# Scores laid out bank by bank with 12 matmuls per group, first queries in two loads, and VectorE exponentials in every sixth chunk

## The chip, the cores and the metric

One core of a Trainium2 chip runs the whole kernel. The metric is the device time of one execution in microseconds (us). Ratios compare versions on the same chip and in the same rounds. Spans in the profile are some 1.7 us shorter than the times.

## The reference

```python
B, Hq, Hkv, Sq, Sk, D = 16, 32, 8, 288, 512, 128      # bf16 q, k, v
k = jnp.repeat(k, rep, axis=1); v = jnp.repeat(v, rep, axis=1)   # rep = 4
scores = jnp.einsum("bhqd,bhkd->bhqk", q, k) * D ** -0.5
p = softmax(scores, axis=-1)
return jnp.einsum("bhqk,bhkd->bhqd", p, v)
```

The four query heads of one key head make a group: 128 groups of 4 x 288 = 1152 query rows, which are NT = 9 tiles of 128, against NJ = 4 key tiles of 128. A group has 36 blocks of 128 x 128 scores, or 4608 score columns, and is worked on in NC = 3 chunks of CH = 1536 columns, which are three banks each of PSUM, the memory that matmuls write to. There are NS = 384 chunks.

## The kernel before

Each step n of TensorE makes the scores of chunk n and the value matmuls of chunk n - 3. ScalarE takes the exponentials of a chunk in one instruction. In every ninth chunk VectorE takes the last 120 columns instead, by a polynomial in eight small operations. Row sums come from a column of ones beside the values, and VectorE divides as it evicts, that is, as it moves the results out of PSUM. Condensed, with comments added and lines left out:

```python
TPC = 3; BANK = 512; CH = TPC * BANK; LAG = 3; W = 120; EVERY = 9; FIRST_SHARED = 4
NPT = 6                                   # probability buffers; score buffers: 2
TW = TPC * P                              # 384: a chunk is [key tile j][3 query tiles]
cuts = sorted(set(range(0, CH + 1, BANK)) | set(range(0, CH + 1, TW)))
pieces = [(c, c // TW, c % TW, e - c) for c, e in zip(cuts[:-1], cuts[1:])]   # 384 128 256 256 128 384

def op_s(n):                              # scores of chunk n
    waits = [have("k", g), have_q(g, i)]
    if n >= 2: waits.append(("s_e", n - 1))            # exponential n-2 done: buffer free
    for x, (c, j, r0, w) in enumerate(pieces):
        if shared(n) and c + w == CH: w -= W           # the last W go elsewhere, by op_sy
        ins = matmul(ps_s[:, n % 2, c:c + w], kt_sb[..., j, gi, :], qg[:, r0:r0 + w])

def op_pv(r):                             # values of chunk r: 4 key tiles x 3 query tiles
    waits = [("s_vc", g + 1), ("s_e", r + 1), ("s_ev", r - 1)]
    ...
def op_q0(i):                             # first queries: three loads of three tiles
    c0, c1 = i * TPC, (i + 1) * TPC
    nc.sync.dma_start_transpose(qt_sb[:, 0, c0:c1], q_v[0:P, c0 * D:c1 * D])
# SP: q0(0) q0(1) q0(2) q(1) k(0, groups 2..3) q(2) v(groups 2..3) q(3) ...
# ACT queue: keys of group 0, then of group 1, then values of groups 0 and 1
for n in range(NS):                       # TensorE
    op_s(n)
    if shared(n): op_sy(n)
    if n == 2: op_kt(1, range(NJ), 1)     # transposes of group 1's keys
    if n >= LAG: op_pv(n - LAG)
```

## Time and profile before

| | before |
|---|---|
| time | 525.38 us (525.32 to 526.12, 3 runs) |
| step of TensorE | 1335 ns: scores 655, values 680 |
| ScalarE, one whole chunk, end to end | 1343.5 ns; with VectorE's help 1243 |
| scores of chunk 3 start | 9.07 us |
| from there to the end of the last scores ("steady part") | 508.22 us |

The lines that carry the reading are in the prediction below. Two more groups are useful (line, engine, operation, tiles and shapes, count, then busy us and mean ns of one, then idle time of the engine before them and what ended it): the value matmuls, which the change leaves alone, and VectorE's evictions, which share their engine with the polynomial.

```profile
L418 PE MATMUL ps_o<-v_sb,pt_sb 128*128 128x129 bf16 x4596 | 322.8, 220 | 0.2 <-DVE o_sb L522 0.2
L522 DVE TENSOR_TENSOR o_sb<-ps_o,rl_sb 128x384 bf16<-128x384 f32 x383 | 212.9, 556 | 10.3
```

The 0.2 us is the whole of what value matmuls waited for evictions, and it belongs to the tail.

### The profile page before, as it was taken

The page shows a single profiled execution, that of the slowest core. Times are in us where ns is not written, and L with a number is a line of the kernel's source. Part 1 is how long each engine was busy: PE and PEld are TensorE (multiplying, and loading weights), DVE is VectorE, ACT ScalarE, POOL GpSimd, SP SyncE. Part 2 cuts the span into 40 slices and gives each one's busy share as a digit, 9 for nine tenths or more (in the row PEclk, how much of TensorE's full clock was granted, in tenths as well). Part 3 has the DMA queues.
Part 4 walks back from the last instruction along what each step waited for, and adds up shares of the span by engine and source line. Part 5 has one row for each costly group of instructions (what it writes and reads, how often), then busy time and mean ns, then how long its engine had stood idle before and what let it go on. Part 6 is the DMA issues. An engine that isn't in the chain of part 4 may idle for free.

```text
span 523.5 us, 16876 instructions
## 1 busy us (share of the span) xinstructions
PE 517.6 (99%) x6981; PEld 459.0 (88%) x6981; DVE 339.9 (65%) x1148; ACT 515.1 (98%) x389; POOL 79.6 (15%) x135
## 2 busy tenths in 40 slices
PE   7999999999999999999999999999999999999997
PEld 5888888888888888888888888888888888888886
DVE  2766666666666666666666666666666666666665
ACT  6999999999999999999999999999999999999996
POOL 1111111111111111111111111111111111111110
PEclk9999999999999999999999999999999999999999
DMA  8999999999999999999999999999988999896212
GB/s 167 223 255 246 205 223 252 194 205 245 252 196 275 208 211 248 215 225 219 216 228 221 222 203 252 230 184 246 225 218 211 233 211 201 219 212 178 79 69 92
DMA packets 253147, 110.15 MB, mean 210 GB/s; under 512 B 219792, under 2 KB 236816, under 8 KB 253072
## 3 DMA queue, kind: packets, MB, share of 16 engines
q1 hardware_dynamic: 252512, 108.56, 97.7%
q8 instruction: 55, 0.90, 0.7%
q10 hardware_dynamic: 560, 0.52, 0.4%
q14 instruction: 20, 0.16, 0.1%
HBM read 17.04 MB, written 37.75 MB: 105 GB/s over the span
## 4 chain that ended last, share of the span: by engine, by line
PE 97%; DMA 1%; SPq 1%; DVE 0%; issue 0%
PE ps_o L418 50%; PE ps_s L384 47%; DMA qt_sb<-in_q_dram 1%; SPq L315 1%; PE ps_o L394 0%; DVE o_sb L522 0%; DVE rl_sb L512 0%; DVE o_sb L532 0%; PE ps_o L607 0%; DVE bad_sb L558 0%; DVE flag_i L675 0%; DVE bad_sb L555 0%
## 5 line engine op out<-in xcount | busy, mean ns | idle before, releaser
L453 ACT ACTIVATE pt_sb<-ps_s 128x1536 bf16<-128x1536 f32 (+2 forms) x385 | 512.8, 1455 | 0.6 <-PE ps_s L384 0.5
L418 PE MATMUL ps_o<-v_sb,pt_sb 128*128 128x129 bf16 x4596 | 322.8, 220 | 0.2 <-DVE o_sb L522 0.2
L384 PE MATMUL ps_s<-qt_sb,kt_sb 128*128 128x128 bf16 (+3 forms) x2304 | 312.2, 272 | 1.5 <-DMA qt_sb<-in_q_dram 1.4
L418 PEld LDWEIGHTS ps_o<-v_sb,pt_sb 128*128 128x128 bf16 x4596 | 289.9, 98 | 22.9 <-DVE o_sb L522 0.4
L384 PEld LDWEIGHTS ps_s<-qt_sb,kt_sb 128*128 128x128 bf16 x2304 | 193.4, 98 | 35.6 <-issue 1.0
L522 DVE TENSOR_TENSOR o_sb<-ps_o,rl_sb 128x384 bf16<-128x384 f32 x383 | 212.9, 556 | 10.3
L512 DVE RECIPROCAL rl_sb<-ps_o 128x3 f32<-128x3 f32 x383 | 68.7, 179 | 160.8 <-PE ps_o L418 160.8
L505 POOL COPY v_sb<-vd_sb 128x512 bf16<-128x512 bf16 x128 | 78.7, 615 | 431.6 <-PE ps_o L418 412.2
L486 DVE SCALAR_TENSOR_TENSOR u_sb<-u_sb,m_sb 128x120 f32<-128x120 f32 x84 | 23.4, 278 | 0.0
L493 DVE SCALAR_TENSOR_TENSOR pt_sb<-u_sb,e_sb 128x120 bf16<-128x120 f32 x42 | 12.2, 290 | 1.4
L486 DVE SCALAR_TENSOR_TENSOR u_sb<-m_sb 128x120 f32<-128x120 f32 x42 | 11.6, 277 | 0.0
L464 DVE TENSOR_SCALAR y_sb<-ps_o 128x120 f32<-128x120 f32 x42 | 10.6, 253 | 0.0
L477 DVE TENSOR_SCALAR m_sb<-t_sb 128x120 int32<-128x120 int32 x42 | 9.4, 223 | 1.4
L477 DVE TENSOR_SCALAR e_sb<-t_sb 128x120 int32<-128x120 int32 x42 | 9.5, 226 | 0.0
L394 PE MATMUL ps_o<-qt_sb,kt_sb 128*128 128x120 bf16 x42 | 9.1, 216 | 0.0
L470 DVE TENSOR_SCALAR t_sb<-y_sb 128x120 int32<-128x120 f32 x42 | 9.0, 213 | 0.0
L364 DVE COPY kt_sb<-ps_o 128x512 bf16<-128x512 bf16 x2 | 0.8, 424 | 6.6 <-PE ps_o L357 6.6
L394 PEld LDWEIGHTS ps_o<-qt_sb,kt_sb 128*128 128x128 bf16 x42 | 4.1, 98 | 0.0
L370 PE MATMUL ps_o<-z_sb 128*128 128x512 bf16 (+1 forms) x9 | 2.7, 447 | 1.3 <-DVE z_sb L638 1.3
L548 DVE TENSOR_REDUCE st_sb<-rl_sb 128x1 f32<-128x72 f32 (+1 forms) x16 | 3.5, 217 | 0.0
L550 DVE TENSOR_REDUCE st_sb<-rl_sb 128x1 f32<-128x72 f32 (+1 forms) x16 | 3.5, 216 | 0.0
L447 ACT ACTIVATE pt_sb<-ps_s 128x512 bf16<-128x512 f32 x1 | 0.6, 597 | 2.3 <-PE ps_s L384 2.3
(31 smaller groups left out, 11.6 us busy)
## 6 DMA issues: line engine op xcount, KB each, us to landing
out_dram<-o_sb SPq DMA_DIRECT2D x127, 288.0 KB, 4.0
vd_sb<-in_v_dram SPq DMA_DIRECT2D x31, 512.0 KB, 5.3
qt_sb<-in_q_dram SPq DMA_TRANSPOSE x130, 4.8
kt_sb<-in_k_dram SPq DMA_TRANSPOSE x32, 5.2
out_dram<-o_sb SPq DMA_DIRECT2D x3, 96.0 KB, 1.8
kd_sb<-in_k_dram ACTq DMA_DIRECT2D x2, 128.0 KB, 2.2
vd_sb<-in_v_dram ACTq DMA_DIRECT2D x1, 256.0 KB, 3.0
vd_sb<-in_v_dram SPq DMA_DIRECT2D x1, 256.0 KB, 3.4
```

Source lines behind the costliest of these rows:

```text
L384: ins = emit(eng, waits if x == 0 else [], lambda: eng.matmul(ps_s[:, n % 2, c:c + w], kt_sb[:, sl, j, gi, :], qg[:, r0:r0 + w], start=Tru ...
L394: emit(eng, [("s_ev", n - LAG - 1)], lambda: eng.matmul(ps_o[:, (n - LAG) % 2, BANK - W:BANK], kt_sb[:, (g // UG) % NSLOT, NJ - 1, g % UG, :],
L418: ins = emit(eng, w_x, lambda: eng.matmul(outs(r)[:, a, :], pt_sb[:, r % NPT, j, a * P:(a + 1) * P], v_sb[:, sl, gi * NJ + j, 0:DV], start ...
L453: emit(eng, waits, lambda: eng.activation(d, s, ACTF.Exp, scale=scale)).then_inc(sem["s_e"], 1)
L464: emit(eng, [("s_yb", nth(n) - NB), ("s_pv", n - LAG + 1)], lambda: eng.tensor_scalar(out=y_sb[:, b], in0=ps_o[:, (n - LAG) % 2, BANK - W: ...
L470: emit(eng, [("s_ym", 2 * (nth(n) - NB)), ("s_y", nth(n))], lambda: eng.tensor_scalar(out=t_sb[:, b], in0=y_sb[:, b], scalar1=Y_MUL, scala ...
L477: emit(eng, [("s_yp", nth(n) - NB), ("s_yb", nth(n))], lambda: eng.tensor_scalar(out=dst[:, b], in0=t_sb[:, b], scalar1=mask, scalar2=bits ...
L486: lambda: eng.scalar_tensor_tensor(out=u_sb[:, b, x], in0=src, scalar=QUARTIC[x], in1=m, op0=ALU.add, op1=ALU.mult)
L493: lambda: eng.scalar_tensor_tensor(out=pt_sb[:, n % NPT, NJ - 1, TW - W:TW], in0=u_sb[:, b, 2], scalar=QUARTIC[3], in1=e_sb[:, b].bitcast( ...
L505: emit(eng, waits, lambda: eng.tensor_copy(v_sb[:, sl, gi * NJ:(gi + 1) * NJ, 0:D], vd_sb[:, sl, gi].rearrange("p (j d) -> p j d", d=D))). ...
L512: emit(eng, [("s_pv", r + 1)], lambda: eng.reciprocal(rl_sb[:, TPC * r:TPC * (r + 1)].unsqueeze(2), outs(r)[:, :, D:DV])).then_inc(sem["s_ ...
L522: emit(eng, waits, lambda: eng.tensor_tensor(out=o_sb[:, g % NO, t0:t0 + TPC, :], in0=outs(r)[:, :, 0:D], in1=rl_sb[:, TPC * r:TPC * (r + ...
```

## The change

The diff is shortened ("..."), and its comments are added. The intent is to make the same scores with fewer matmuls, to let ScalarE keep up by giving VectorE more chunks to help in, and to get through the start with one transfer less. Scores of four query tiles against one key tile now fill a bank exactly: eight banks of 512 columns per group, and one bank with the ninth query tile against the four key tiles. A chunk is three consecutive banks. Therefore a value matmul may need exponentials of its own chunk and of the next.

```diff
-    EVERY = 9
+    EVERY = 6
-    FIRST_SHARED = 4
+    FIRST_SHARED = 6
-    TW = TPC * P
+    TB = BANK // P
+    NF = NT // TB * TB
...
-            c0, c1 = i * TPC, (i + 1) * TPC
+            c0, c1 = ((0, TB), (TB, NT))[i]            # first queries: 4 and 5 tiles
...
-        cuts = sorted(set(range(0, CH + 1, BANK)) | set(range(0, CH + 1, TW)))
-        pieces = [(c, c // TW, c % TW, e - c) for c, e in zip(cuts[:-1], cuts[1:])]
+        def place(t, j):
+            b, c = (t // TB * NJ + j, t % TB * P) if t < NF else (NF // TB * NJ + t - NF, j * P)
+            return b // TPC, b % TPC * BANK + c
+        def pieces(i):
+            left = [(place(t, j)[1], j, t, TB * P) for t in range(0, NF, TB) for j in range(NJ) if place(t, j)[0] == i]
+            return left + [(place(t, j)[1], j, t, P) for t in range(NF, NT) for j in range(NJ) if place(t, j)[0] == i]
...
-            waits = [("s_vc", g + 1), ("s_e", r + 1)]
+            waits = [("s_vc", g + 1), ("s_e", g * NC + uses(r % NC) + 1)]
...
-            op_kt(0, range(NJ), 0)
-            op_warm(8, P, ps_s[:, 1])
+            op_kt(0, range(1), 0)                      # first key tile alone, then the other three
+            op_kt(0, range(1, NJ), 1)
+            op_warm(5, P, ps_s[:, 1])
```

Cut: the same change of indices in the reading of the probabilities and in the polynomial's destination, the waits that free a probability buffer, and the copies that go with the split key transposes.

More of the change, by code (lines that the diff above doesn't have):

```diff
@@ L209, in bass_standalone__gqa_softmax__near_ridge_kernel @@
             S("s_o%d" % i)
-        for i in range(NC):
+        for i in range(2):
             S("s_qp%d" % i)
@@ L240, in bass_standalone__gqa_softmax__near_ridge_kernel @@
         kt_sb = main.enter_context(nc.sbuf_tensor("kt_sb", [P, NSLOT, NJ, UG, P], BF16))
-        pt_sb = main.enter_context(nc.sbuf_tensor("pt_sb", [P, NPT, NJ, TW], BF16))
+        pt_sb = main.enter_context(nc.sbuf_tensor("pt_sb", [P, NPT, CH], BF16))
         o_sb = main.enter_context(nc.sbuf_tensor("o_sb", [P, NO, NT, D], BF16))
@@ L318, in have_q @@
             if g == 0:
-                return ("s_qp%d" % i, 16)
+                return ("s_qp%d" % min(i, 1), 16)
             return ("s_q%d" % (g % NQ), 16 * (g // NQ + (0 if g % NQ == 0 else 1)))
@@ L325, in have @@
             if u == 0 and kind == "k":
-                return ("s_k%d" % min(g, 2), (1, 1, 16)[min(g, 2)])
+                return ("s_k%d" % min(g, 2), (2, 1, 16)[min(g, 2)])
             if u == 0:
@@ L345, in stored, with uses, used, pt @@
             return [("s_o%d" % (g % NO), 16 * (g // NO + 1)) for g in range(NG - NO, LASTG)] + [("s_ol", 16 * NC)]
-        cuts = sorted(set(range(0, CH + 1, BANK)) | set(range(0, CH + 1, TW)))
-        pieces = [(c, c // TW, c % TW, e - c) for c, e in zip(cuts[:-1], cuts[1:])]
+        def place(t, j):
[4 more added lines that the diff above has]
+            return left + [(place(t, j)[1], j, t, P) for t in range(NF, NT) for j in range(NJ) if place(t, j)[0] == i]
+        def uses(b):
+            return max(place(t, j)[0] for t in range(b * TPC, (b + 1) * TPC) for j in range(NJ))
+        def used(i):
+            return max(b for b in range(NC) for t in range(b * TPC, (b + 1) * TPC) for j in range(NJ) if place(t, j)[0] == i)
+        def pt(g, t, j):
+            i, c = place(t, j)
+            return pt_sb[:, (g * NC + i) % NPT, c:c + P]
         def op_kt(g, tiles, bank):
@@ L379, in op_s @@
                 waits.append(("s_e", n - 1))
-            qg = qt_sb[:, g % NQ, i * TPC:(i + 1) * TPC].rearrange("d t p -> d (t p)")
-            for x, (c, j, r0, w) in enumerate(pieces):
+            qg = qt_sb[:, g % NQ].rearrange("d t p -> d (t p)")
+            todo = pieces(i)
+            for x, (c, j, t, w) in enumerate(todo):
                 if shared(n) and c + w == CH:
                     w -= W
-                ins = emit(eng, waits if x == 0 else [], lambda: eng.matmul(
-                    ps_s[:, n % 2, c:c + w], kt_sb[:, sl, j, gi, :], qg[:, r0:r0 + w], start=True, stop=True))
+                w_x = waits if x == 0 else []
+                if n == 0 and x < 2:
+                    w_x = [("s_k0", 1), waits[1]] if x == 0 else waits[:1]
+                ins = emit(eng, w_x, lambda: eng.matmul(
+                    ps_s[:, n % 2, c:c + w], kt_sb[:, sl, j, gi, :], qg[:, t * P:t * P + w], start=True, stop=True))
                 if n == 0 and c + w == BANK:
@@ L392, in op_sy @@
             eng = nc.tensor
-            g, t = n // NC, n % NC * TPC + TPC - 1
+            g = n // NC
+            (t, j), = [(t, j) for t in range(NT) for j in range(NJ) if place(t, j) == (n % NC, CH - P)]
             emit(eng, [("s_ev", n - LAG - 1)], lambda: eng.matmul(
-                ps_o[:, (n - LAG) % 2, BANK - W:BANK], kt_sb[:, (g // UG) % NSLOT, NJ - 1, g % UG, :],
+                ps_o[:, (n - LAG) % 2, BANK - W:BANK], kt_sb[:, (g // UG) % NSLOT, j, g % UG, :],
                 qt_sb[:, g % NQ, t, P - W:P], start=True, stop=True))
@@ L415, in op_pv @@
                     w_x = waits if a == 0 and j == 0 else []
-                    if a == TPC - 1 and j == NJ - 1 and shared(r):
-                        w_x = w_x + [("s_yp", nth(r))]
+                    t = r % NC * TPC + a
+                    i, c = place(t, j)
+                    if c == CH - P and shared(g * NC + i):
+                        w_x = w_x + [("s_yp", nth(g * NC + i))]
                     ins = emit(eng, w_x, lambda: eng.matmul(
-                        outs(r)[:, a, :], pt_sb[:, r % NPT, j, a * P:(a + 1) * P],
+                        outs(r)[:, a, :], pt(g, t, j),
                         v_sb[:, sl, gi * NJ + j, 0:DV], start=(j == 0 and a == 0), stop=(j == NJ - 1),
@@ L429, in op_pv_last @@
                 ins = emit(eng, [("s_e", NS + (0 if a < TPC - 1 else 1))], lambda: eng.matmul(
-                    outs(NS - 1)[:, a, :], pt_sb[:, (NS - 1) % NPT, j, a * P:(a + 1) * P],
+                    outs(NS - 1)[:, a, :], pt(LASTG, NT - TPC + a, j),
                     v_sb[:, sl, gi * NJ + j, 0:DV], start=(j == 0), stop=(j == NJ - 1)))
@@ L439, in op_exp @@
             if n >= NPT:
-                waits.insert(0, ("s_pv", n - NPT + 1))
-            dst, src = pt_sb[:, n % NPT], ps_s[:, n % 2].rearrange("p (j r) -> p j r", r=TW)
-            parts = [(dst.rearrange("p j r -> p (j r)"), ps_s[:, n % 2])]
+                m = n - NPT
+                waits.insert(0, ("s_pv", m // NC * NC + used(m % NC) + 1))
+            d, s = pt_sb[:, n % NPT], ps_s[:, n % 2]
+            parts = [(0, CH)]
             if shared(n):
-                parts = [(d[:, 0:CH - W], s[:, 0:CH - W]) for (d, s) in parts]
+                parts = [(0, CH - W)]
             if n == 0:
-                d, s = parts[0]
                 emit(eng, [("s_s0", 1)], lambda: eng.activation(d[:, 0:BANK], s[:, 0:BANK], ACTF.Exp, scale=scale))
-                parts = [(d[:, BANK:CH], s[:, BANK:CH])]
+                parts = [(BANK, CH)]
             if n == NS - 1:
-                w = TW - P
-                parts = [(dst[:, :, 0:w], src[:, :, 0:w]), (dst[:, :, w:TW], src[:, :, w:TW])]
+                parts = [(0, CH - BANK), (CH - BANK, CH)]
+            parts = [(d[:, a:e], s[:, a:e]) for (a, e) in parts]
             for (d, s) in parts:
@@ L491, in op_yp @@
             eng, b = nc.vector, nth(n) % NB
-            emit(eng, [("s_pv", n - NPT + 1), ("s_ym", 2 * nth(n)), ("s_yu", 3 * nth(n))],
+            emit(eng, [("s_pv", (n - NPT) // NC * NC + used((n - NPT) % NC) + 1), ("s_ym", 2 * nth(n)), ("s_yu", 3 * nth(n))],
                  lambda: eng.scalar_tensor_tensor(
-                     out=pt_sb[:, n % NPT, NJ - 1, TW - W:TW], in0=u_sb[:, b, 2], scalar=QUARTIC[3],
+                     out=pt_sb[:, n % NPT, CH - W:CH], in0=u_sb[:, b, 2], scalar=QUARTIC[3],
                      in1=e_sb[:, b].bitcast(FP32), op0=ALU.add, op1=ALU.mult)).then_inc(sem["s_yp"], 1)
@@ L560, in op_over @@
                 op0=ALU.is_lt, op1=ALU.add)).then_inc(sem["s_bad"], 1)
-        first = [lambda i=i: op_q0(i) for i in range(NC)]
+        first = [lambda i=i: op_q0(i) for i in range(2)]
         first += [lambda: op_q(1), lambda: op_k(0, 2), lambda: op_q(2), lambda: op_v(0, None, 2, UG), lambda: op_q(3)]
@@ L640, in _ @@
             eng.memset(one_f[:], 1.0)
-            op_kc(0, range(NJ), 0, 1)
-            op_kc(1, range(NJ), 1, 2)
+            op_kc(0, range(1), 0, 1)
+            op_kc(0, range(1, NJ), 1, 2)
+            op_kc(1, range(NJ), 1, 3)
             per_b = G * NC
```

## The prediction

> **What bounds the kernel now.** I read the page's rows of busy time and its chain first, then the groups by shape, then the chain piece by piece in the steady part, and the start and the end last. Two engines look full:
>
> ```profile
> PE 517.6 (99%) x6981; PEld 459.0 (88%) x6981; DVE 339.9 (65%) x1148; ACT 515.1 (98%) x389; POOL 79.6 (15%) x135
> ...
> PE 97%; DMA 1%; SPq 1%; DVE 0%; issue 0%
> ```
>
> So the bound is TensorE or ScalarE, within a per cent, and the chain says TensorE. The work is 384 chunks of 1536 score columns: 3 per group, 128 groups. In each step TensorE makes the scores of chunk n (6 matmuls) and then the 12 probability-by-value matmuls of chunk n-3, while ScalarE takes the exponentials of a chunk. The rows by shape:
>
> ```profile
> L453 ACT ACTIVATE pt_sb<-ps_s 128x1536 bf16<-128x1536 f32 x340 | 461.5, 1467 | 0.6 <-PE ps_s L384 0.5
> L384 PE MATMUL ps_s<-qt_sb,kt_sb 128*128 128x384 bf16 x726 | 236.7, 326 | 1.5 <-DMA qt_sb<-in_q_dram 1.4
> L384 PE MATMUL ps_s<-qt_sb,kt_sb 128*128 128x128 bf16 x768 | 168.2, 219 | 0.0
> L384 PE MATMUL ps_s<-qt_sb,kt_sb 128*128 128x256 bf16 x768 | 146.6, 273 | 0.0
> L394 PE MATMUL ps_o<-qt_sb,kt_sb 128*128 128x120 bf16 x42 | 9.1, 216 | 0.0
> ```
>
> Durations of pipelined matmuls overlap, so the chain's pieces are the better measure of a step (start, length, what):
>
> ```profile
> 33.27 0.66 PE ps_s L384 x6
> 33.92 0.68 PE ps_o L418 x12
> 34.60 0.60 PE ps_s L384 x6
> 35.20 0.05 PE ps_o L394
> 35.26 0.68 PE ps_o L418 x12
> ```
>
> From the starts of single matmuls in the trace, one to the next: 162.5 ns after a 384-column one, 109.1 after 256, 55.9 after 128, 56.7 after 129 columns. The six scores take 2 x 162.5 + 2 x 109.1 + 2 x 55.9 = 655 ns and the twelve others 680; steps start 1335 ns apart, always, and the engine's idle time in the steady part is 0. Which engine leads is seen on ScalarE: each exponential begins a constant 49 ns after the modelled end of the last score matmul, and starts too are 1335 ns apart. But its single durations climb over eight chunks from 1444 to 1494 ns, and drop to 1402 when VectorE takes 120 columns (every ninth chunk). ScalarE's ends are thus 1343.5 ns apart: alone it is slower than TensorE. After the shared chunk it has caught up. Over nine chunks ScalarE needs 8 x 1343.5 + 1243 = 11,991 ns and TensorE 12,018, so TensorE leads by 27 ns in 12,018. The score buffers are double, so the next but one chunk still finds its buffer free about 300 ns early. A faster TensorE alone could gain only those 27 ns per nine chunks before ScalarE leads, 1.2 us in all; beyond that the two must go down together.
>
> The start is the second place. TensorE idles until the queries of group 1 have landed:
>
> ```profile
> 0.82 3.90 SPq L315 DMA_TRANSPOSE qt_sb<-in_q_dram  x3
> 4.77 1.43 SPq L310 DMA_TRANSPOSE qt_sb<-in_q_dram  x1
> ...
> 7.16 0.81 PE L384 MATMUL ps_s<-qt_sb,kt_sb 128*128 128x384 bf16 x6 [0.58 <-DMA qt_sb<-in_q_dram]
> 7.81 0.39 PE L357 MATMUL ps_o<-ident,kd_sb 128*128 128x128 bf16 x4
> 9.07 0.81 PE L384 MATMUL ps_s<-qt_sb,kt_sb 128*128 128x384 bf16 x6 [0.87 <-DMA qt_sb<-in_q_dram]
> ```
>
> From 9.07 us on, the scores of chunk 3, TensorE never stops until the tail at 518.5.
>
> **What the Trainium skill says.** "TensorE: Matmul & The Clock Gate", section "Wait — 56ns, not 53.3ns?": a warm matmul of N columns is followed by the next after N / 2.4 GHz plus about 2.5 ns, whatever N is (55.6 ns at 128 columns, 215.7 at 512). The trace agrees: 55.9, 109.1 and 162.5 are 53.3, 106.7 and 160 plus 2.4 to 2.6. "PSUM — Partial Sum Buffer", "The four PSUM rules": one matmul's output stays within one bank of 512 fp32 columns. That is why the old layout, 384 columns per key tile, had to be cut six times over three banks. "ScalarE: Activation LUTs", "What ACT_TABLE_LOAD costs": 0.833 ns per column, with successive ACTIVATEs overlapping. The trace has (1343.5 - 1243) / 120 = 0.84. "DMA: Bandwidth & Descriptors", "Issuing engines are not separate DMA queues": a second issuer saves only issue time, and all transfers share the 16 DMA engines; in the trace the first piece of the queries landed 1.2 us after its issue ended and the second, with keys and values under way, 2.1.
>
> **The change part by part.**
> Score matmuls. A group's 36 blocks of 128 columns are laid out anew: eight banks of one key tile by four query tiles (512 columns) and one bank with the ninth query tile (4 x 128). Per group that is 8 + 4 = 12 matmuls against 18, with the same 4608 columns. With 215.8 ns for 512 (213.3 + 2.5; the trace of before has no warm one), chunks 0 and 1 of a group cost 647.5 ns, chunk 2 costs 431.6 + 223.6 = 655. The mean is 650, a saving of 5 ns a step: 6 matmuls x 128 groups x 2.5 ns = 1.92 us. Everything lies on TensorE's path. From chunk 3 to chunk 383 it is 380 steps: 1.9 us.
>
> Sharing. 62 chunks instead of 42 (chunks 6, 12, ... 372). On TensorE a shared chunk has one more matmul, 20 x 2.5 ns = +0.05 us. On ScalarE each saves 100.5 ns, 2.0 us in all, which does not come off the end, but lets ScalarE follow: per six chunks 5 x 1343.5 + 1243 = 7960 ns, against TensorE's 6 x 1330 + 2.5 = 7983. TensorE still leads by 23 ns. With the old sharing ScalarE's 11,991 per nine chunks would have stood against TensorE's 11,973, so the new matmuls would have been held up by about 2 ns a step (0.8 us in all). VectorE pays eight small operations a chunk, 2.04 us by the sum of their rows, 20 x 2.04 = 41 us more on an engine busy for 340 of 523. Beside the matmuls, it has room: in a shared step its evictions end at least 0.8 us before TensorE wants the accumulator again, and 1.0 us elsewhere.
>
> New dependences. Values of query tiles now need exponentials of the next chunk (tile 0's last key tile is in chunk 1). The value matmuls of chunk n-3 come right after the scores of chunk n, which themselves waited for exponential n-2, so nothing waits longer. The probability buffers are freed one step later than before; with six of them the exponential wants one two steps after that.
>
> Start. Three query loads become two (4 and 5 tiles). Each of the three took 1.23 to 1.31 us to issue, and the whole of group 1 with nine tiles 1.43, so the issue hardly depends on size, and group 1 is issued 1.25 us earlier. The bytes stay, and the DMA engines are busy from 4 us on, so I count 1.1 us: landing at 7.8 instead of 8.94. Then other waits take its place: the second load, five tiles, lands perhaps 0.2 to 0.4 later than 5.49, so the exponential of chunk 1 begins at about 6.7 instead of 6.44 and ends near 8.2, and the keys of group 1 must be transposed and copied (8.24 to 8.66 before), which follows the scores of chunk 2, near 6.8 instead of 7.16, so at about 8.3. Chunk 3 starts at about 8.4 instead of 9.07: 0.7 us. The first key tile copied alone makes the first exponential 0.2 us earlier, which is ahead of the other waits and worth nothing by itself.
>
> Tail. The last chunk is still split into 1024 and 512 columns. The next to last value matmuls now need the first of these, done at 518.42 in the old trace; they waited until 518.84 for VectorE's eviction anyway. So 0.
>
> Sum: -1.92 + 0.05 - 0.7 = -2.6 us. 525.4 becomes 522.8, half a per cent.
>
> **The rivals.**
> 1. ScalarE becomes the bound. For: it is within 23 ns in 7983 of TensorE. Against: sharing every sixth chunk has been sized for it. If its 1536 columns took 1350 instead of 1343.5, six chunks would be 7993, and 10 ns x 64 = 0.6 us would be lost: 523.4. At the start its backlog also grows till chunk 6 (before: chunk 4), worth 0.1 to 0.3.
> 2. VectorE's chains, half as often again, hold up TensorE through evictions. Now the copy of the values on GpSimd falls in the same step as the chain's beginning. It ran beside 125 evictions that took 558 ns against 555, so only an operation after the first 0.65 us could suffer. A stall of 100 ns in each of 62 chains would cost 6 us: 529.
> 3. The start gains nothing, for the transfers end when they did: 523.5. Or the whole 1.25 us comes through: 522.2.
>
> **Range and chances.** The matmul term rests on four spacings that agree to 0.2 ns, and I trust it to 0.3 us. The start is good for 0.3 to 1.2. Rival 1 can take 0.6. The runs of before lie within 0.8 of one another. So 521.9 to 524.1. Two per cent is 10.5 us, four times what is on offer, and only rival 2 many times over would lose as much.
>
> **What would show it.** Score matmuls of 512 columns 216 ns apart, and steps 1327, 1327, 1335 ns apart. Exponentials whose durations climb by some 14 ns a chunk and drop after each sixth. No idle time of TensorE between 9 and 515 us. Chunk 3's scores between 8.0 and 8.7 us. VectorE's busy time near 375 us. The prediction is wrong if TensorE's chain shows waits for exponentials or evictions in the steady part, or if 512-column matmuls are further apart than 216 ns.

## The result, and the profile after

The changed kernel took 523.09 us (median of 4 runs, 522.91 to 524.22) beside 525.69 (525.32 to 526.12, 4 runs). The ratio is 0.9955, with a 95% interval of 0.9938 to 0.9972: faster, but by less than 2%. Ratios here are the mean time of one kernel's runs over that of the other's of the same rounds, so not quite the ratio of the medians. Over all runs the kernel before has a median of 525.51 us (31 runs) and the changed one of 523.00 (14 runs): 2.5 us less.

The page of the first profiled run after, busy rows and chain:

```profile
PE 510.6 (98%) x6124; PEld 395.5 (76%) x6230; DVE 363.0 (69%) x1309; ACT 513.4 (98%) x389; POOL 79.8 (15%) x135
...
PE 96%; DMA 1%; issue 1%; SPq 0%; DVE 0%
```

Read with care: 6124 matmuls stand beside 6230 weight loads, so 106 matmul records are missing from this trace. Part of the "issue" in its chain is those holes. A second profile of the same kernel, taken for the first experiment, has all of them. Its groups of the score matmuls and exponentials:

```profile
L481 ACT ACTIVATE pt_sb<-ps_s 128x1536 bf16<-128x1536 f32 x320 | 437.1, 1470 | 0.1
...
L409 PE MATMUL ps_s<-qt_sb,kt_sb 128*128 128x512 bf16 x962 | 271.0, 380 | 0.8 <-DVE kt_sb L385 0.6 <-DMA qt_sb<-in_q_dram 0.3
...
L409 PE MATMUL ps_s<-qt_sb,kt_sb 128*128 128x128 bf16 x512 | 49.5, 219 | 0.0
...
L409 PE MATMUL ps_s<-qt_sb,kt_sb 128*128 128x392 bf16 x62 | 20.4, 329 | 0.0
```

962 + 62 + 512 = 1536 score matmuls (and 62 of 120 columns) have taken the place of 2304. The chain of that profile, piece by piece in the steady part (start, length, what):

```profile
33.35 0.68 PE ps_o L446 x12
34.03 0.65 PE ps_s L409 x3
34.67 0.68 PE ps_o L446 x12
35.35 0.66 PE ps_s L409 x6
36.01 0.68 PE ps_o L446 x12
36.69 0.60 PE ps_s L409 x3
37.29 0.05 PE ps_o L420
37.34 0.68 PE ps_o L446 x12
```

Three matmuls of 512 take 0.65 us where six took 0.66; two of 512 with four of 128 take 0.66. In single starts, 512-column matmuls are 215.8 ns apart, and the steps are 1327.5, 1327.5 and 1335 ns long (a shared chunk adds 2.5), 1330.4 on average. The value matmuls take 680 ns as before. The time went out of the steps: the steady part, from the start of chunk 3's scores to the modelled end of chunk 383's, is 506.36 us, in each of three profiles of the changed kernel (the second and the third ran on different chips), against 508.22. That is 1.86 us.

The start did not go as in the median in the first profile (the slowest of its four runs). Its loads and the first wait of TensorE, on the timeline (start, length, engine and line; a query load's length is the time that its issue took; in brackets the idle time before and what ended it):

```profile
0.82 2.64 SPq L316 DMA_TRANSPOSE qt_sb<-in_q_dram  x2
3.51 1.39 SPq L311 DMA_TRANSPOSE qt_sb<-in_q_dram  x1
...
9.88 0.81 PE L409 MATMUL ps_s<-qt_sb,kt_sb 128*128 128x512 bf16 x3 [1.89 <-DMA qt_sb<-in_q_dram]
```

Group 1's queries were issued at 3.51 us instead of 4.77, yet they landed at 9.74 instead of 8.94. The values of groups 0 and 1, on the other queue, landed at 9.56 instead of 6.28. In the second profile:

```profile
3.51 2.26 SPq L311 DMA_TRANSPOSE qt_sb<-in_q_dram  x1
...
8.59 0.81 PE L409 MATMUL ps_s<-qt_sb,kt_sb 128*128 128x512 bf16 x3 [0.56 <-DVE kt_sb L385]
```

There the queries landed at 8.38, and the last wait before chunk 3 is for the copy of group 1's keys. The tail, from the start of the last chunk's exponential to the end of the span, is 6.17 to 6.19 us before and after.

### The profile page after: what moved, and what is told of

The parts are those of the page before. It is cut to its first block, busy times and chain, and to the rows that moved or that the text cites. A ratio compares the mean times of both kernels' runs of the same rounds, so it can differ in the third digit from the quotient of the medians.

```text
span 522.5 us, 15279 instructions
## 1 busy us (share of the span) xinstructions
PE 510.6 (98%) x6124; PEld 395.5 (76%) x6230; DVE 363.0 (69%) x1309; ACT 513.4 (98%) x389; POOL 79.8 (15%) x135
## 4 chain that ended last, share of the span: by engine, by line
PE 96%; DMA 1%; issue 1%; SPq 0%; DVE 0%
PE ps_o L446 50%; PE ps_s L409 45%; DMA qt_sb<-in_q_dram 1%; PE ps_o L420 1%; SPq L316 0%; DVE o_sb L550 0%; DVE rl_sb L540 0%; DVE o_sb L560 0%; PE ps_o L636 0%; DVE bad_sb L586 0%; DVE flag_i L705 0%; DVE bad_sb L583 0%
## 5 line engine op out<-in xcount | busy, mean ns | idle before, releaser
L446 PEld LDWEIGHTS ps_o<-v_sb,pt_sb 128*128 128x128 bf16 x4596 | 283.7, 98 | 49.9 <-DVE o_sb L550 0.4
L409 PE MATMUL ps_s<-qt_sb,kt_sb 128*128 128x512 bf16 (+2 forms) x1430 | 290.6, 320 | 6.4 <-DMA qt_sb<-in_q_dram 1.9
L409 PEld LDWEIGHTS ps_s<-qt_sb,kt_sb 128*128 128x128 bf16 x1536 | 124.0, 98 | 63.5 <-ACT pt_sb L481 2.2
L514 DVE SCALAR_TENSOR_TENSOR u_sb<-u_sb,m_sb 128x120 f32<-128x120 f32 x124 | 34.5, 278 | 0.0
L521 DVE SCALAR_TENSOR_TENSOR pt_sb<-u_sb,e_sb 128x120 bf16<-128x120 f32 x62 | 17.5, 283 | 2.1
L514 DVE SCALAR_TENSOR_TENSOR u_sb<-m_sb 128x120 f32<-128x120 f32 x62 | 17.2, 277 | 0.0
L492 DVE TENSOR_SCALAR y_sb<-ps_o 128x120 f32<-128x120 f32 x62 | 15.7, 253 | 0.0
L505 DVE TENSOR_SCALAR m_sb<-t_sb 128x120 int32<-128x120 int32 x62 | 13.8, 223 | 2.1
L420 PE MATMUL ps_o<-qt_sb,kt_sb 128*128 128x120 bf16 x62 | 13.4, 216 | 0.0
L498 DVE TENSOR_SCALAR t_sb<-y_sb 128x120 int32<-128x120 f32 x62 | 13.2, 213 | 0.0
```

The lines of the kernel that those rows point to most:

```text
L409: ins = emit(eng, w_x, lambda: eng.matmul(ps_s[:, n % 2, c:c + w], kt_sb[:, sl, j, gi, :], qg[:, t * P:t * P + w], start=True, stop=True))
L420: emit(eng, [("s_ev", n - LAG - 1)], lambda: eng.matmul(ps_o[:, (n - LAG) % 2, BANK - W:BANK], kt_sb[:, (g // UG) % NSLOT, j, g % UG, :], ...
L446: ins = emit(eng, w_x, lambda: eng.matmul(outs(r)[:, a, :], pt(g, t, j), v_sb[:, sl, gi * NJ + j, 0:DV], start=(j == 0 and a == 0), stop=( ...
L492: emit(eng, [("s_yb", nth(n) - NB), ("s_pv", n - LAG + 1)], lambda: eng.tensor_scalar(out=y_sb[:, b], in0=ps_o[:, (n - LAG) % 2, BANK - W: ...
L498: emit(eng, [("s_ym", 2 * (nth(n) - NB)), ("s_y", nth(n))], lambda: eng.tensor_scalar(out=t_sb[:, b], in0=y_sb[:, b], scalar1=Y_MUL, scala ...
L505: emit(eng, [("s_yp", nth(n) - NB), ("s_yb", nth(n))], lambda: eng.tensor_scalar(out=dst[:, b], in0=t_sb[:, b], scalar1=mask, scalar2=bits ...
```

## The experiments

Eleven runs followed, five rounds each: nine new kernels, and the changed one twice. All gave correct results. The kernel before measured 525.33, 525.66 and 525.61 us. "Steady" and "chunk 3" are from each kernel's profiled run.

| kernel | time, us | ratio to before | chunk 3 at, us | steady, us |
|---|---|---|---|---|
| before (first profile) | 525.69 | 1 | 9.07 | 508.22 |
| after (first profile) | 523.09 | 0.9955 | 9.88 | 506.36 |
| after again | 522.92 | 0.9953 | 8.59 | 506.36 |
| 512 cut into 2 x 256 | 525.64 | 1.0003 | 8.86 | 508.90 |
| after, sharing of before | 523.36 | 0.9963 | 8.56 | 506.86 |
| before, sharing of after | 525.35 | 0.9999 | 9.26 | 508.27 |
| after, three query loads | 523.48 | 0.9957 | 9.48 | 506.37 |
| before, two query loads | 525.13 | 0.9986 | 8.98 | 508.22 |
| after, nothing shared | 527.80 | 1.0044 | 8.70 | 510.96 |
| after, every third shared | 523.28 | 0.9950 | 8.80 | 506.52 |
| after, control | 523.20 | 0.9956 | 8.62 | 506.36 |
| after, keys earlier | 523.07 | 0.9955 | 8.79 | 506.43 |
| and values later | 522.96 | 0.9953 | 7.96 | 506.88 |

### 1. The changed kernel again

No edit.

> The changed kernel unchanged, for its spread and for a second profile of its start. In its first profile the queries of group 1, issued 1.26 us earlier than before, landed 0.8 us later (9.74 against 8.94 us), so that run lost 0.8 us at the start and won 1.9 us in the steady part; its time, 524.22, was the slowest of four (the others 522.91 to 523.22). Theory A (the landing at the start varies from run to run): the median of many runs is again near 523.0, and this profile shows the scores of chunk 3 at another time than 9.88 us, probably 8.3 to 9, with a time lower by the same amount. Theory B (the late landing belongs to the kernel): chunk 3 at 9.8 to 9.9 us again, and the time does not follow it. Either way the steady part, from the scores of chunk 3 to those of chunk 383, is 505.6 to 505.8 us.

Measured: 522.92 us (522.78 to 523.16), chunk 3 at 8.59, steady 506.36. (The expectation counted to the start of chunk 383's scores: that is 505.54, just under its 505.6 to 505.8.) The time followed the start: 1.28 us earlier at chunk 3, 1.28 us less in the time of that run (522.94 against 524.22). So the late landing of the first profile is a matter of the run and not of the kernel. Why one execution is late was not found.

### 2. The same layout with more matmuls

```diff
+            left = [(c + h * 256, j, t + 2 * h, 256) for (c, j, t, _) in left for h in range(2)]
-                if n == 0 and x < 2:
+                if n == 0 and x in (0, 2):
```

> The changed kernel with each 512-column score matmul cut into two of 256: same layout, sharing and start, 20 score matmuls a group in place of 12. Theory A (the steady gain is a fixed 2.5 ns per matmul): 8 x 128 x 2.5 = 2.6 us slower than the changed kernel, so about 525.6, the time of the kernel before; steps 6.7 ns longer, the starts of 256-column matmuls 109 ns apart. Rival (the gain comes from the layout or the banks and not from the number of matmuls): the time of the changed kernel, 523.1.

Measured: 525.64 us, ratio to before 1.0003 (0.9990 to 1.0017). Its group of score matmuls, and its chain in one stretch:

```profile
L410 PE MATMUL ps_s<-qt_sb,kt_sb 128*128 128x256 bf16 x1986 | 280.6, 273 | 0.7 <-DVE kt_sb L386 0.6 <-DMA qt_sb<-in_q_dram 0.2
```

```profile
300.50 0.66 PE ps_s L410 x8
301.16 0.68 PE ps_o L447 x12
```

The steady part is 2.54 us longer than the changed kernel's, for 1024 more matmuls: 2.5 ns each. Starts after 256 columns are 109.1 ns apart, as in the kernel before. The layout, the sharing and the start are those of the change, and the steady gain is gone. It was the number of matmuls. Each of them brings its own weight load (7254 of each in this trace), so the 2.5 ns are shown for the pair of a matmul and its load; no run separates the two.

### 3. The change with the old sharing

```diff
-    EVERY = 6
-    FIRST_SHARED = 6
+    EVERY = 9
+    FIRST_SHARED = 4
```

> The changed kernel with the sharing of before (every ninth chunk from chunk 4). Theory A (ScalarE needs 1343.5 ns for a whole chunk and 1243 for a shared one): ScalarE becomes the bound, 11,991 against 11,973 ns per nine chunks, so steps are 1332.3 ns on average instead of 1330.6 and the time is 0.6 to 0.8 us above the changed kernel's, 523.8; TensorE shows idle time before score matmuls that exponentials end, up to 0.8 us in sum. Rival (ScalarE has slack that its profile hides): TensorE never waits and the time is that of the changed kernel or 0.05 less.

Measured: 523.36 us, 0.44 above the changed kernel in the same call; steady 0.50 longer. ScalarE's ends are 1343 ns apart for whole chunks and 1244 for shared ones, 1332.2 on average, and TensorE's steps have grown to 1331.7 from 1330.4. ScalarE is the bound here. Two things were expected differently. The loss is 0.5 and not 0.8, because the double buffer is slack that must be used up first (experiment 5 shows how much). Single exponentials last about 1510 ns at the beginning and level off at 1660 to 1740 only after some 100 chunks. The mean tells the same:

```profile
L481 ACT ACTIVATE pt_sb<-ps_s 128x1536 bf16<-128x1536 f32 x340 | 469.3, 1670 | 0.0
```

against 1470 in the changed kernel. And TensorE's wait is shown by no view: the list of waits has the start alone. A delay of a few ns a step hides in matmuls whose modelled durations overlap. It is seen in the spacing of starts only, and in the backlog on the engine that it waits for. So one sign that the prediction named for its being wrong, waits for exponentials in TensorE's chain, is blind to a bound of this size.

### 4. The old layout with the new sharing

```diff
-    EVERY = 9
-    FIRST_SHARED = 4
+    EVERY = 6
+    FIRST_SHARED = 6
```

> The kernel before with the sharing of the change (every sixth chunk from chunk 6), all else old. Theory A (TensorE was the bound): nothing gained, +0.05 us for 20 more small matmuls, so a ratio of 1.000 within 0.001; steps stay 1335 ns. Rival (ScalarE was the bound): up to 2.0 us gained, 523.7. A third, that VectorE's longer chains hold up TensorE, would show as a time above 526 and idle time of TensorE ended by evictions.

Measured: 525.35 us, ratio 0.9999 (0.9986 to 1.0013), steady 508.27: 0.05 more. Taking 2 us of work from ScalarE moved nothing, so ScalarE was not the bound before. With 3 this settles the pair: the sharing alone is worth nothing, and it saves 0.5 us of what the matmuls gain.

### 5. No sharing

```diff
-    FIRST_SHARED = 6
+    FIRST_SHARED = 600
```

> The changed kernel with no chunk shared: ScalarE takes all columns. Theory A (a whole chunk costs ScalarE 1343.5 ns, and it is then the bound): steps of 1343.5 ns, 13.2 ns a step over the changed kernel, 376 to 383 steps: 5.0 us more, 527.9. Rival 1 (back-to-back ACTIVATEs cost what the skill's formula gives, 93 + 1536 x 0.833 = 1372.5 ns): 16 us more, 539. Rival 2 (ScalarE only follows TensorE and has slack): 522.8.

Rival 1 is an estimate from the Trainium skill, "ScalarE: Activation LUTs", section "What ACT_TABLE_LOAD costs" (186 ns plus 0.833 per column, less an overlap of 93).

Measured: 527.80 us, steady 4.6 us longer than the changed kernel's: theory A's 5.0 in all but 0.4, where rival 1 would have meant 16. ScalarE's ends are 1343.3 ns apart on average over 330 chunks. Its exponentials stand in line, each 1752 ns from start to end:

```profile
L481 ACT ACTIVATE pt_sb<-ps_s 128x1536 bf16<-128x1536 f32 x382 | 513.4, 1752 | 0.0
```

1343.3 is 12.9 ns above the changed kernel's mean step of 1330.4, and over 380 steps that makes 4.9; 0.3 us of it went into the buffers' slack. The slack can be seen: the durations climb from 1445 ns to 1765 in some 30 chunks and then stay between 1761 and 1770, so the backlog is full at 0.32 us. TensorE again shows no wait for an exponential in the steady part. Instead the first 512-column matmul of a chunk is followed by the next after 224 ns on average instead of 216, and the first score matmul starts 62 ns (median) after the last value matmul instead of 57.

### 6. Twice as many chains on VectorE

```diff
-    EVERY = 6
+    EVERY = 3
```

> The changed kernel with every third chunk shared (124 chunks instead of 62), to see how far VectorE's load can grow. The 20 chains that the change added raised VectorE's busy time by 23 us (340 to 363), 1.15 us a chain beside the evictions. Theory A (VectorE is off the path with room to spare): 62 more chains make it busy some 434 of 521 us, TensorE pays 62 x 2.5 ns = 0.16 us, and the time is 523.1. Rival 2 of the prediction (the chains delay evictions until TensorE waits for its accumulator): TensorE idles before value matmuls, and the time rises by 62 x 0.1 us and more, above 529.

Measured: 523.28 us, steady 506.52, which is 0.16 more than the changed kernel's, the whole of it being the 62 extra matmuls.

```profile
PE 510.0 (98%) x6181; PEld 398.6 (76%) x6292; DVE 436.4 (84%) x1805; ACT 513.2 (98%) x389; POOL 79.8 (15%) x135
```

VectorE busy 436 us of 522 still holds nothing up. The prediction's second rival falls with room to spare.

### 7. Three loads in the new kernel, two in the old

```diff
# the changed kernel
-            c0, c1 = ((0, TB), (TB, NT))[i]
+            c0, c1 = ((0, TB), (TB, NF), (NF, NT))[i]
# the kernel before
-            c0, c1 = i * TPC, (i + 1) * TPC
+            c0, c1 = ((0, TPC), (TPC, NT))[i]
```

The waits of the chunks follow the loads.

> The changed kernel with the first queries in three loads (4, 4 and 1 tiles) instead of two (4 and 5); the steady part is untouched. Theory A (one issue less lets group 1's queries be issued 1.25 us and land about 0.5 us earlier, which is the start's gain): group 1 is issued at 4.8 us again and lands at 8.9 to 9.1, chunk 3's scores start at 9.1 instead of 8.59, and the time is 0.4 to 0.5 us above the changed kernel: 523.4. Rival (the start's gain comes from the key tile copied alone or from the new order of the first chunks, not from the number of loads): chunk 3 at about 8.6 and 522.9.

> The kernel before with the first queries in two loads (3 and 6 tiles) instead of three; all else old. Theory A: the start's gain alone: group 1 lands near 8.4, chunk 3's scores start near 8.6 instead of 9.07, held then by the copy of group 1's keys, and the time is 0.4 to 0.5 us less: 524.9; its steady part stays 508.2 us. Rival: no gain, 525.3.

Measured, three loads in the new kernel: 523.48 us; group 1's queries issued at 4.76 and landed at 9.35 (expected: 8.9 to 9.1), chunk 3 at 9.48 (expected: 9.1). The wait and its end, on the timeline:

```profile
4.76 1.91 SPq L311 DMA_TRANSPOSE qt_sb<-in_q_dram  x1
...
9.48 0.81 PE L409 MATMUL ps_s<-qt_sb,kt_sb 128*128 128x512 bf16 x3 [0.78 <-DMA qt_sb<-in_q_dram]
```

Measured, two loads in the old kernel: 525.13 against 525.66 us, ratio 0.9986 (0.9972 to 0.9999), so a gain that the interval only just sets apart from none. Its profile shows chunk 3 at 8.98, held by the copy of the keys, as expected, but 0.4 us later than expected:

```profile
8.98 0.82 PE L384 MATMUL ps_s<-qt_sb,kt_sb 128*128 128x384 bf16 x6 [0.56 <-DVE kt_sb L364]
```

In the profiles with three loads (before, old layout with new sharing, this one) group 1's queries landed at 8.94, 9.13 and 9.35 us; in those with two and the values on ScalarE's queue at 8.17, 8.37, 8.38, 8.48, 8.53, 8.57, 8.65, 8.76 and, once, 9.74. The loads are worth some 0.5 us of the start both ways, by these landings. The times alone show less: in the new kernel the ratio to before is 0.9957 (0.9943 to 0.9970) with three loads and 0.9953 to 0.9956 with two, which the intervals do not tell apart, and the changed kernel did not run in the same call.

### 8. Mending the start

The control is the changed kernel. The first edit moves the transposes of group 1's keys from behind chunk 2's scores to behind chunk 1's. The second also takes the first values off ScalarE's queue.

```diff
-                if n == 2:
+                if n == 1:
                     op_kt(1, range(NJ), 1)
# the second, in addition
-            op_v(0, eng, 0, 2)
-        first += [lambda: op_q(1), lambda: op_k(0, 2), lambda: op_q(2), lambda: op_v(0, None, 2, UG), ...]
+        first += [lambda: op_q(1), lambda: op_v(0, None, 0, 1), lambda: op_k(0, 2), lambda: op_q(2),
+                  lambda: op_v(0, None, 1, 2), lambda: op_v(0, None, 2, UG), ...]
```

> The changed kernel once more, beside the next two on the same chip, and for a third profile of its start. Chunk 3's scores begin between 8.5 and 9.9 us (8.59 and 9.88 so far); the steady part is 506.36 us as twice before; 522.9 to 523.2.

> The changed kernel with the transposes of group 1's keys right after the scores of chunk 1 instead of after those of chunk 2. Theory A (in the runs where its queries land in time, chunk 3 waits 0.6 us for the copy of these keys): the copy is done a microsecond earlier, and chunk 3 begins right after its queries land, about 0.1 us (landing 8.4) to 0.5 us (landing 8.0 or earlier) sooner: 522.6 to 522.9. Rival (the landing alone decides): the control's time within 0.1 us.

> The same, and the first values of groups 0 and 1 leave ScalarE's queue: group 0's go out on the queue of the queries behind group 1's queries, and group 1's later still. Theory A (the 256 KB of values contend with the queries at the start): the second load of queries lands at 5.3 to 5.5 us instead of 5.3 to 6.1, group 1's by 7.6, chunk 3's scores begin at 8.0 and the time is 0.5 us under the control: 522.4. Rival (the values are then late themselves): the first value matmul waits for them, 9.3 us or later, and the gain is taken back; TensorE idles before it.

Measured: control 523.20, keys earlier 523.07, values later too 522.96 us; the ranges of the three overlap. Control first, then keys earlier, on the timeline (the six score matmuls of chunks 0 and 1, and those of chunk 3):

```profile
4.34 2.23 PE L409 MATMUL ps_s<-qt_sb,kt_sb 128*128 128x512 bf16 x6
...
8.62 0.81 PE L409 MATMUL ps_s<-qt_sb,kt_sb 128*128 128x512 bf16 x3 [0.62 <-DMA qt_sb<-in_q_dram]
```

```profile
4.34 2.91 PE L409 MATMUL ps_s<-qt_sb,kt_sb 128*128 128x512 bf16 x6
...
8.79 0.82 PE L409 MATMUL ps_s<-qt_sb,kt_sb 128*128 128x512 bf16 x3 [0.44 <-ACT pt_sb L481]
```

With the keys earlier, chunk 3 at 8.79 waited for the exponential of chunk 1, which began at 7.29 in that run, against 6.79 in the control. The second query load explains little of that: it landed at 5.83 against 5.69. The rest is the matmuls of chunk 1, which started 400 and 427 ns apart against 241 and 216. When the matmuls double their rate, from 427 ns for 512 columns to 216, differs from run to run: at 5.8 us in the control and 7.0 here. What sets it no run shows; PEclk, the granted clock, reads 1.00 throughout. The copy of the keys was one of three waits that end within a few tenths, so removing it alone is worth nothing. With the values later, the queries did land at 7.54 and chunk 3 began at 7.96, the earliest of all. About half of that lead is chance: in this profile the rate had doubled by 4.9 us, so that the exponential of chunk 1, on which chunk 3 waited last, began at 6.45 instead of 6.79. Then the rival came true, on the timeline:

```profile
7.96 0.82 PE L409 MATMUL ps_s<-qt_sb,kt_sb 128*128 128x512 bf16 x3 [0.29 <-ACT pt_sb L481]
8.96 0.85 PE L446 MATMUL ps_o<-v_sb,pt_sb 128*128 128x129 bf16 x12 [0.18 <-POOL v_sb L533]
```

The scores take 0.65, so the first values began 0.35 us late, and a second wait for values at 13.10 cost 0.14 more; its steady part is 0.51 longer. Most of the gain was taken back: 522.96 where 522.4 was expected. No version is shown to beat the changed kernel beyond the spread of its own runs.

## Why the prediction was right

**Steady part: right in mechanism and in size.** The sum had -1.92 + 0.05 for the whole, -1.87. Measured between chunk 3 and the last scores: -1.86. The predicted spacing of 216 ns and the steps 1327, 1327, 1335 came out. The 2.5 ns per matmul, which the prediction carried over from 128, 256 and 384 columns to 512, was confirmed from the other side by the split (1024 matmuls, 2.54 us). "Four spacings that agree to 0.2 ns" is one too many: the fourth, 56.7 ns for 129 columns, is 2.9 over, but the change leaves those matmuls alone.

**ScalarE: right.** 1343.5 and 1243 ns were read off the climbing durations, a reading that might have been an artefact of the trace. The kernel without sharing measured 1343.3 directly. In the changed kernel the durations run 1445, 1453, 1467, 1480 and then 1393 at the shared chunk, which is the climb and drop that the prediction named. The loss without the new sharing was put at 0.8 us and is 0.5: the term left out the slack of the score buffers, some 0.3 us, which a backlog fills once. (The prediction had read this slack itself, as a buffer free "about 300 ns early".) The faster matmuls alone, with the old sharing, gained 1.36 us (508.22 to 506.86) where 1.2 was predicted. The backlog at the start, put at 0.1 to 0.3 us in rival 1, cost nothing: in the second profile the durations reach 1625 ns at chunk 17, short of the full 1765, and the steady part is 506.36 as in the control, where they lie under 1500 up to chunk 378.

**VectorE: right that it is off the path, too high in its busy time.** 375 us was forecast (the prediction's own sum, 340 + 41, is 381), 363 measured. Adding 20 x 2.04 us counted each small operation in full, though their recorded times overlap (one begins at 12.92 us and takes 0.22, the next begins at 13.06); a chain raises the busy time by 1.15 us.

**Start: right in the difference, in part by luck, and wrong in its parts.** The forecast was 0.7 us at chunk 3, from 9.07 to 8.4. The steady part takes 1.86 of the 2.5 us between the medians of all runs, which leaves 0.65 for the start. But both ends of the forecast were early. The single profile of before was an early one: its run took 525.22 against the median of 525.51. In the changed kernel chunk 3 began at 8.59 and 8.62 in two profiles and at 9.88 in one, which lies outside the 8.0 to 8.7 that was named as a sign. That two shifts of 0.2 to 0.3 us cancel is luck. The step that was mis-sized is the landing of group 1's queries, put at 7.8 us; in the three profiles it was 8.38, 8.48 and 9.74. The issue came 1.26 us earlier, as worked out, and the landing only about 0.6 (by the profiles listed in experiment 7, without the late one). That other transfers hold it up is likely but rests on one profile: issued at the same 3.51 us without the values on the other queue, it landed at 7.54 (experiment 8). "The first exponential 0.2 us earlier" seems not to have come, 5.01 against 5.04 us, but that is again the early profile: there the first score matmuls, at 4.6 us, ran at the full rate already, while in the changed kernel's they started 427 ns apart. Against the two other profiles with the old start of the keys (experiment 4, and two loads in 7), 5.33 us, it is 0.3. The prediction counted nothing on it.

**Tail and new dependences: right.** Nothing waits longer; the tail is within 0.02 us.

The total, 522.8 predicted and 523.09 measured, lies in the range. The rival of an unchanged start (523.5) is wrong for the median of all runs, 523.00; the slowest run, 524.22, lies above it and just outside the range.

## What to carry to other kernels

When two engines are full within a few tenths of a per cent, take each one's own period: from the spacing of starts on the engine that never waits, and from the ends of the one whose durations climb. Then relieve both, and check with one experiment for each alone. Judge by these spacings and not by the list of waits, which here showed nothing of a bound that cost 4.6 us. A fixed cost of 2.5 ns per matmul was worth a change of layout here because TensorE was full all the time; it bought 0.35%. And read gains at the start of a kernel from many runs: here one landing moved by over a microsecond from one execution to another (8.38 to 9.74 us), and removing one of three waits that end together gained nothing.

## What the Trainium skill lacked or had wrong

- "ScalarE: Activation LUTs", "What ACT_TABLE_LOAD costs": the slope of 0.833 ns per column held (0.84 from 1343.5 and 1243). The fixed part between back-to-back ACTIVATEs did not: 186 ns less an overlap of about 93 gives an estimate of 1373 ns for 1536 columns, where 1343.3 was measured over 330 in a row, so 63 ns of fixed cost. One that found the engine idle (chunk 3 of the kernel before) took 1451, where the page's sum gives 1466.
- "TensorE: Matmul & The Clock Gate": the 2.5 ns per warm matmul, given there for 128 and 512 columns, held for 256 and 384 too, and for 120, 264 and 392. At 129 columns the spacing was 56.7, which is 2.9 over 129 / 2.4.
- "Perfetto Trace Analysis", which says that TensorE's ends are estimated, does not say what follows: a wait of 13 ns a step (4.6 us in all, experiment 5) appears in no wait of the views and not in the chain. Nor does it say that matmul records can be missing (106 of 6230 here), which then look like gaps.
- "DMA: Bandwidth & Descriptors": no section gives the issue time of a transposing load from HBM by size (one figure in cycles stands there, for small tiles). Here loads of 1, 3, 4, 5 and 6 tiles took 1.23 to 1.33 us to issue and loads of 9 tiles from 1.25 to 4.1. Nor does it say how far a landing can wander: the same load of the same kernel landed at 8.38, 8.48 and 9.74 us.
